# K0, K1 and Q0 on two DMA queues, weights' high words scaled in place, emission by data labels, first layer's units set between the weights' conversions

## The chip, the cores and the metric

The kernel runs on one core of a Trainium2 chip. Its engines run side by side, each through its own list of instructions in order: PE (TensorE, matmuls), DVE (VectorE), ACT (ScalarE), POOL (GpSimd) and SP (SyncE, which here issues DMAs). The metric is the device time of one execution in microseconds (us), lower is better. Three runs of the kernel before took 696.23, 696.32 and 696.54 us; the median is 696.32.

## What is computed

A delta-rule recurrence over 768 tokens, for 32 independent heads of 48 columns, followed by a feed-forward layer with a gate.

```python
k_n = k / (np.linalg.norm(k, axis=-1, keepdims=True) + 1e-06)
for t in range(S):                                  # S = 768, 32 heads, D = 48
    y[:, :, t] = np.einsum('bhd,bhde->bhe', q[:, :, t], state)
    v_old = np.einsum('bhde,bhd->bhe', state, kt)
    state = state + bt[:, :, :, None] * np.einsum('bhd,bhe->bhde', kt, vt - v_old)
...
h = x @ w_in                                        # 3072 x 384 @ 384 x 2048
sp = np.where(h > 20.0, h, np.log1p(np.exp(np.minimum(h, 20.0))))
g = h * np.tanh(sp)
return (g @ w_out).astype(np.float32)               # @ 2048 x 384
```

The two weight matrices come as 64-bit floats. They are read as pairs of 32-bit words and are turned on the chip into two f32 parts each (a high part and a remainder).

## The kernel before

The 768 tokens are cut into 12 chunks (n = 0 to 11) of 64. For each chunk the heads' recurrence is solved in closed form by small matmuls, and the chunk's output, 256 rows of 384, then goes through the feed-forward layer. A chunk's layer is called unit n here; it has eight pieces (fp = 0 to 7) of 18 matmuls `h<-x,wi` (L575), eight steps of the gate that alternate between ACT and DVE (L588 to L595), and 12 matmuls `acc<-wo,g` (L610).

Work ahead of a unit:

- `early(g)` for two chunks 2g and 2g+1: K is loaded (`ksrc`), transposed on DVE into `kt` (L264), multiplied with itself on PE (`pg`, L283), masked into `d` (L286), transposed into `gt` (L294); norms and the factor nb follow (L302 to L328), and then a triangular inverse is built row by row on DVE, for the groups g = 0 and 1 in 14 pairs of multiply (`pr`, L336) and add (`gt`, L338). It ends in three rows, `gt` times `bp` (L340) and the transposes `tt` (L345) and `tu` (L349).
- `merge(n)` for n up to 3: it joins two 16-row halves of the inverse, with PE matmuls `ma` (L375) and `mb` (L386), ACT copies `ym`, a DVE add (L389) and a transpose `tn` (L391).
- the stages of chunk n (all matmuls at L433): `gq`, `ta`, `tb`, `pz`, `py`/`ps`, each of them evacuated by ACT or DVE before the next. `turn_q` (L421) brings Q in transposed. The state of a chunk goes from `ps` into the next one.
- `turn(n)` transposes the chunk's output (`xt`, L548) into the layer's input x, of a high part (ACT, L550) and a remainder (DVE, L552). The first `h` of unit n waits for x.

The weights are 28 parts (12 `ri` of 128x1024 words, 16 `ro` of 128x768). `convert` takes for each: an ACT row that reads the high words (L219), four DVE rows (L221 to L227), the ACT rounding (L230), two PE matmuls for the remainder (`loi` or `loo`, L238 and L241) and the ACT copy of it (L243).

The order of emission is a plan: each generator is put into a heap with times from the table TN, and the piece with the least time is emitted next. Up to time 90 of the plan the framework's own scheduler sets the order in which each engine's instructions stand; from then on PE's order is that of the plan. All loads are issued by SP, in one order. K0 is loaded before K1, and Q0 goes into the buffer of K1 after it is transposed. In the trace the first `h` of units 0, 1, 2 and 3 start at 98.5, 170.2, 237.2 and 284.6 us; the stretches between these times are called stages below.

Of the kernel before, what the change touches and what calls it, by code (L numbers as in the profile page):

```python
# [10 lines left out]
F32 = mybir.dt.float32  # L11
# [9 lines left out]
F64_LEAST = 2.0 ** -15  # L21
F64_MOST = 122879.9921875
# [7 lines left out]
def bcast_in(ap, n):  # L30

    return ap.unsqueeze(2).broadcast_to([ap.shape[0], ap.shape[1], n])


@with_exitstack
def kernel(
# [40 lines left out]
    P = 128  # L77
# [28 lines left out]
    def put(gen, *times):
        for t in times:
            heappush(plan, (t, next(count), gen))

    def one(f, *a):  # L110
        f(*a)
        yield
# [8 lines left out]
    def defer(wait, f, *a):  # L121
        put(one(f, *a), now[0] + wait)
# [44 lines left out]
    loaded = []  # L167

    def load(dst, src):

        m = nc.sync.dma_start(out=dst, in_=src)  # L171
# [12 lines left out]

# [17 lines left out]
    identr = mp.tile([P, NCH, UT], F32R, tag="x0", name="identr", bufs=2)[:, 0, 0:P]  # L202
    spare = mp.tile([P, NCH * UT], F32, tag="x1", name="spare", bufs=2)[:, :512]
    nc.vector.tensor_copy(identr, ident)

    def convert(kind, i):
# [4 lines left out]
        if k % 3 < 2 or k >= 21:  # L211
# [7 lines left out]
        nc.scalar.activation(a, high.bitcast(F32), AF.Abs, scale=2.0 ** -80)  # L219
        yield  # L220
        nc.vector.tensor_scalar(a, a, F64_LEAST * 2.0 ** -80, F64_MOST * 2.0 ** -80, op0=ALU.max, op1=ALU.min)  # L221
# [599 lines left out]
```

## Time and profile before

| | |
|---|---|
| median of three runs | 696.32 us (696.23 to 696.54) |
| span of the profiled execution | 694.4 us, so about 1.9 us of the time lies around it |
| PE, DVE, ACT, POOL busy | 92%, 69%, 63%, 7% of the span |
| HBM moved | 31.56 MB read, 4.72 MB written |

The profile lists, for one execution, when each instruction started and how long it took, and the idle time before it with what ended it. "issue" is idle time for which the profile shows no other instruction to wait for. PEclk is the granted share of the PE clock. In a row "x60" counts records, and a matmul on 32-bit floats leaves two records each.

### The profile page before, as it was taken

To read this page: it belongs to the slowest core of one execution; us is meant where nothing else is said; L and a number is where in the kernel's file an instruction comes from. 1 tells how busy PE (TensorE), PEld (TensorE's weight loads), DVE (VectorE), ACT (ScalarE), POOL (GpSimd) and SP (SyncE) were. 2 spreads that over 40 slices of the span, in tenths; PEclk is the share of its full clock that TensorE was granted. 3 is DMA by queue.
4 is the path that set the end of the run, shared out by engine and by line. 5 is a ranking of instruction groups with operands and counts; after the bars stand their busy time and mean duration, and the time that the engine had idled before them with its cause. 6 is when DMAs were issued, how large, how long until landed. Compare 5 with 4: busy or idle time off the path is not lost.

```text
span 694.4 us, 23260 instructions
## 1 busy us (share of the span) xinstructions
PE 636.3 (92%) x10163; PEld 584.6 (84%) x10163; DVE 478.3 (69%) x1048; ACT 440.0 (63%) x821; POOL 48.8 (7%) x84
## 2 busy tenths in 40 slices
PE   6543899889979899999999999999999999999997
PEld 3313776779879899999899999999999999999997
DVE  4795278995449986579984699965899745453442
ACT  1350368775635766866758857568667587777674
POOL 5000000100101001000010010010000100000000
PEclk9565589999899999999999999999999999999999
DMA  5999230113041341231322403312222121000000
GB/s 82 227 247 348 39 59 14 21 17 59 18 62 25 45 70 32 33 66 26 48 47 36 70 15 48 59 33 33 44 35 43 19 37 35 13 19 8 1 24 24
DMA packets 160934, 37.79 MB, mean 54 GB/s; under 512 B 154176, under 2 KB 157248, under 8 KB 160832
## 3 DMA queue, kind: packets, MB, share of 16 engines
q1 hardware_dynamic: 160832, 36.30, 26.6%
q8 instruction: 80, 1.31, 0.8%
q14 instruction: 22, 0.18, 0.1%
HBM read 31.56 MB, written 4.72 MB: 52 GB/s over the span
## 4 chain that ended last, share of the span: by engine, by line
PE 45%; DVE 25%; ACT 13%; issue 6%; SPq 6%; DMA 3%; POOL 0%; DVEq 0%; ACTq 0%; POOLq 0%
PE h L575 16%; PE acc L610 15%; SPq L171 6%; DVE e L593 4%; PE gq L433 3%; ACT e L591 3%; DVE g L595 3%; DVE pr L336 3%; DVE gt L338 2%; ACT e L590 2%; ACT e L592 2%; PE py L433 2%; DVE e L589 2%; DVE xx L421 2%; DVE xx L480 2%
## 5 line engine op out<-in xcount | busy, mean ns | idle before, releaser
L575 PE MATMUL h<-x,wi 128*128 128x256 f32 x1728 | 228.6, 286 | 4.3 <-DVE e L593 3.5
L575 PEld LDWEIGHTS h<-x,wi 128*128 128x128 f32 x1728 | 215.9, 190 | 10.5 <-DVE e L593 2.8
L610 PE MATMUL acc<-wo,g 128*128 128x384 f32 x1152 | 222.1, 342 | 0.3 <-issue 0.3
L610 PEld LDWEIGHTS acc<-wo,g 128*128 128x128 f32 x1152 | 199.2, 189 | 3.8 <-issue 0.7
L593 DVE SCALAR_TENSOR_TENSOR e<-e,h 128x512 f32<-128x512 f32 x96 | 65.8, 686 | 97.0 <-ACT e L592 93.7
L590 ACT ACTIVATE e<-e 128x512 f32<-128x512 f32 x96 | 60.6, 631 | 73.2 <-DVE e L589 72.8
L594 ACT CAST g<-e 128x512 fp32r<-128x512 f32 x96 | 59.5, 620 | 41.2 <-DVE e L593 40.6
L595 DVE TENSOR_TENSOR g<-e,g 128x512 fp32r<-128x512 f32 x96 | 65.2, 679 | 20.6 <-ACT g L594 19.4
L588 ACT ACTIVATE e<-h 128x512 f32<-128x512 f32 x96 | 57.1, 595 | 30.8 <-PE h L575 30.0
L591 ACT ACTIVATE e<-e 128x512 f32<-128x512 f32 x96 | 60.5, 631 | 2.6
L592 ACT ACTIVATE e<-e 128x512 f32<-128x512 f32 x96 | 60.6, 632 | 2.4
L589 DVE TENSOR_SCALAR e<-e 128x512 f32<-128x512 f32 x96 | 40.8, 425 | 26.5 <-ACT e L588 26.2
L338 DVE TENSOR_TENSOR gt<-gt,pr 128x84 f32<-128x84 f32 (+14 forms) x148 | 46.1, 311 | 3.2
L336 DVE TENSOR_TENSOR pr<-gt 128x84 f32<-128x84 f32 (+14 forms) x148 | 46.0, 311 | 2.5
L433 PE MATMUL gq<-xx,kt 64*64 64x112 f32 (+1 forms) x768 | 45.2, 266 | 0.9 <-ACT wo L243 0.9
L433 PEld LDWEIGHTS py<-xx 128*64 128x64 f32 x768 | 39.1, 143 | 6.5 <-issue 2.8
L480 DVE TENSOR_TENSOR xx<-gq,amask 64x256 f32<-64x256 f32 x96 | 40.1, 418 | 4.6 <-PE gq L433 3.9
L433 PE MATMUL py<-xx 128*64 128x48 f32 x768 | 43.2, 230 | 0.0
L433 PEld LDWEIGHTS gq<-xx,kt 64*64 64x64 f32 x768 | 38.6, 141 | 2.6 <-issue 1.2
L414 POOL TENSOR_TENSOR vt<-vt,ne 128x384 f32<-128x384 f32 x24 | 21.0, 880 | 278.1 <-DVE ne L328 123.3
L433 PE MATMUL pz<-vt,tt 64*64 64x48 f32 x768 | 38.3, 236 | 2.4 <-ACT tt L462 1.3
L433 PEld LDWEIGHTS pz<-vt,tt 64*64 64x64 f32 x768 | 34.7, 140 | 6.4 <-ACT tt L462 2.8
(112 smaller groups left out, 717.9 us busy)
## 6 DMA issues: line engine op xcount, KB each, us to landing
ri<-in_moe_w_in_dram SPq DMA_DIRECT2D x12, 512.0 KB, 5.5
ro<-in_moe_w_out_dram SPq DMA_DIRECT2D x16, 384.0 KB, 6.0
vt<-in_v_dram SPq DMA_DIRECT2D x48, 96.0 KB, 2.8
xx<-in_k_dram SPq DMA_DIRECT2D x48, 96.0 KB, 2.8
out_dram<-o SPq DMA_DIRECT2D x48, 96.0 KB, 2.9
qsrc<-in_q_dram SPq DMA_DIRECT2D x48, 64.0 KB, 2.5
ksrc<-in_k_dram SPq DMA_DIRECT2D x44, 64.0 KB, 2.8
qsrc<-in_q_dram SPq DMA_DIRECT2D x48, 32.0 KB, 2.4
```

Of the source, the lines that this page charges most:

```text
L336: nc.vector.tensor_tensor(out=pv, in0=nj, in1=xj, op=ALU.mult)
L338: nc.vector.tensor_tensor(out=below, in0=below, in1=pv, op=ALU.add)
L433: last[:] = [nc.tensor.matmul(*a, start=True, stop=True)]
L575: nc.tensor.matmul(h[:, f2, :], wt["i", f * P // WI * NCH + c][:, i2, f0:f0 + P], x[:, c, :], start=(i == 0), stop=(i == 3 * NCH - 1))
L588: for d, f in ((0.7, lambda: nc.scalar.activation(e, h, AF.Exp, scale=-1.0)), (0.55, lambda: nc.vector.tensor_scalar(e, e, EXP20, 1.0, op0 ...
L590: (0.65, lambda: nc.scalar.activation(e, e, AF.Square)),
L591: (0.65, lambda: nc.scalar.activation(e, e, AF.Ln, bias=0.5, scale=0.5)),
L592: (0.7, lambda: nc.scalar.activation(e, e, AF.Exp, scale=-1.0)),
L593: (0.8, lambda: nc.vector.scalar_tensor_tensor(e, e, -1.0, h, op0=ALU.add, op1=ALU.mult)),
L594: (0.7, lambda: nc.scalar.copy(out=gg[:, 0], in_=e)),
L595: (0.8, lambda: eng.tensor_tensor(out=gg[:, 1], in0=e, in1=gg[:, 0], op=ALU.subtract))):
L610: nc.tensor.matmul(acc[t], gg[:, a, f2, ts_], wt["o", f][:, i2, :], start=(f == 0 and i == 0), stop=(f == NF - 1 and i == 2))
```

## The change

- **Two queues.** `load_src` puts half of the DMAs of K0, K1 and Q0 on ACT's queue, half stay on SP's. Q0 has a buffer of its own, `q0`, and is loaded straight after K1, before beta. The load of ACT's function table comes after these 12 DMA issues on ACT. The first weights are loaded behind beta and no longer between K0 and K1.
- **High words scaled in place.** `convert`'s first ACT row multiplies the high words by 2^-112 where they lie; the clamp on DVE then reads them there, every second word, from both sides (-F64_MOST to F64_MOST); the sign is merged by other bit operations. There are still an ACT row and four DVE rows for each part.
- **Emission by labels.** A piece of the plan can name data that it needs (`need`) and gives a label when its data is made (`give`); a piece whose needs aren't there is held until the label comes. TT holds new times of single pieces. Up to time 122 of the plan all five engines now stand in the plan's order.
- **Units between conversions.** Unit 0's pieces are put at `u0(fp)`, times that follow the conversions of the parts they read. `merge(1)` comes after unit 0 has begun. K2's and K3's `kt` come later, among the conversions. `early(0)`'s steps have no conversion between them.
- **Small ones.** 107 `warm` matmuls on zeros (before 23) keep PE at work; the identity is made first on POOL; all memsets of `ksrc` and `qsrc` are on DVE; `ym0` lies in the place of the last weight part; `tu` is transposed ahead of `tt` in groups 0 and 1; in chunk 0 `gq` takes the `acc` banks of PSUM; chunk 1's second `pz` and chunk 2's first `gq` are separate stages.

The core of the diff:

```diff
+    'early2': [118.5, 147.9, 150.3, 155.1, 164.7, 165.034, ...
+    'cv0': [None, 37.464, 38.114, 38.764, 39.414, 40.164, 40.964, 41.564],
...
-              d0=["k0",1,"k1","b",3,"q",3,"v","x",4,"k2",4,"k3",13],
-              us=[76., 140., 192., 242.],
-              warm=[(0.5,14),(16.5,3),(18.,6)],
+              fixed=((122.,('PE','DVE','Activation','Pool','SP')),(1e9,('PE',))),
+              d0=["k0","k1","q","a","b",3,"v","x",4,"k2","k3",7,"p",14],
+              us=[49., 136., 184., 232.],
+              warm=[(0.5,13),(8.0,2),(11.5,66),(27.9,2),(29.5,4),(30.6,4),(32.2,2),(36.4,4),(40.2,3),(42.1,2),(43.6,2),(46.6,3)],
...
-        m = nc.sync.dma_start(out=dst, in_=src)
-        if loaded and len(loaded) < TN.get('lo', 150):
-            order(m, loaded[-1])
-        loaded.append(m)
+        m = (nc.scalar if turns[0] else nc.sync).dma_start(out=dst, in_=src)
...
-    def load_src(dst, src, n):
+    def load_src(dst, src, n, both=False):
         for hh in range(2):
+            turns[0] = both and hh == 1
...
-        nc.scalar.activation(a, high.bitcast(F32), AF.Abs, scale=2.0 ** -80)
-        yield
-        nc.vector.tensor_scalar(a, a, F64_LEAST * 2.0 ** -80, F64_MOST * 2.0 ** -80, op0=ALU.max, op1=ALU.min)
+        nc.scalar.mul(out=high.bitcast(F32), in_=high.bitcast(F32), mul=2.0 ** -112)
+        yield
...
+        nc.vector.tensor_scalar(a, high.bitcast(F32), -F64_MOST, F64_MOST, op0=ALU.max, op1=ALU.min)
         yield
         nc.vector.tensor_scalar(ai, ai, 3, None, op0=ALU.logical_shift_left)
         yield
-        nc.vector.scalar_tensor_tensor(ai, high, 0x7FFFFFFF, ai, op0=ALU.bitwise_or, op1=ALU.bitwise_and)
+        nc.vector.scalar_tensor_tensor(ai, high, -0x80000000, ai, op0=ALU.bitwise_and, op1=ALU.bitwise_or)
...
+    def u0(fp):
+        return when(7 * (fp // 2) + 2.9 + 2.8 * (fp % 2)) + TN['ul']
...
-        put(one(units[n][0], fp), us(n + (fp + 0.25) / NFP))
+        put(f"g1.{n}.{fp}", one(units[n][0], fp), us(n + (fp + 0.25) / NFP) if n else u0(fp),
+            need=[f"X{n}.{t}" for t in range(2)] + [f"Wi{fp * 2 * P // WI * NCH + c}" for c in range(NCH)])
...
     def run(until):
         while plan and plan[0][0] < until:
-            now[0], _, gen = heappop(plan)
-            next(gen, None)
+            piece = heappop(plan)
+            now[0], _, gen, *at_piece[:2] = piece
+            lacks = [x for x in needs[gen] if x not in given]
+            if lacks:
+                waiting.setdefault(lacks[0], []).append(piece)
+                continue
+            at_piece[2] = 0
+            needs[gen] = next(gen, None) or ()
```

What stands where, at three places. DVE in the middle of `early(0)`'s steps (`pr` and `gt`); `mi` and `spare` are conversions of weights. Before:

```order
L221 TENSOR_SCALAR mi_808<-mi_808 128x512
L227 SCALAR_TENSOR_TENSOR mo_739<-ro_261,mo_739 128x384
L338 TENSOR_TENSOR gt_414<-gt_414,pr_3_458 128x2x12x3
L223 TENSOR_SCALAR mi_808<-mi_808 128x512
L336 TENSOR_TENSOR pr_4_461<-gt_414 128x88
L221 TENSOR_SCALAR spare<-spare 128x512
L225 SCALAR_TENSOR_TENSOR mi_808<-ri_273,mi_808 128x512
L338 TENSOR_TENSOR gt_414<-gt_414,pr_4_461 128x2x11x4
```

The same steps of the change on DVE, from the first one on:

```order
L410 TENSOR_TENSOR pr_1_506<-gt_482 128x28
L412 TENSOR_TENSOR gt_482<-gt_482,pr_1_506 128x2x14
L410 TENSOR_TENSOR pr_2_509<-gt_482 128x52
L412 TENSOR_TENSOR gt_482<-gt_482,pr_2_509 128x2x13x2
L410 TENSOR_TENSOR pr_3_512<-gt_482 128x72
L412 TENSOR_TENSOR gt_482<-gt_482,pr_3_512 128x2x12x3
```

The conversions have left this place; the first of them now stands behind the evacuation of chunk 0's first `gq`.

PE at chunk 0's stages before: `merge(1)` (its `ma` and `mb`) and a conversion's remainder (`loi`) stand between `pz` and the first `py`.

```order
L433 MATMUL pz_1_862<-vt_1_266,tt_106 64x48 x15
L375 MATMUL ma_0_884<-tu_501,d_165 32x16 x18
L375 MATMUL ma_1_920<-tu_501,d_165 32x16 x32
L238 MATMUL loi_955<-spare,ident 128x512
L241 MATMUL loi_955<-wi_953,identr 128x512
L386 MATMUL mb_0_961<-tt_106,ym_503 32x16 x32
L386 MATMUL mb_1_996<-tt_106,ym_503 32x16 x32
L433 MATMUL py_0_1036<-xx_98 64x48 x2
```

PE of the change behind unit 0's first piece `h_0`, where `merge(1)` now stands:

```order
L665 MATMUL h_0_1028<-x_0_1005,wi_986 128x256
L301 MATMUL loo_1056<-mo_1015,identr 128x384
L304 MATMUL loo_1056<-wo_1054,identr 128x384
L454 MATMUL ma_0_1062<-tu_556,d_177 32x16 x32
L454 MATMUL ma_1_1097<-tu_556,d_177 32x16 x32
L465 MATMUL mb_0_1135<-tt_111,ym_115 32x16 x32
L301 MATMUL loo_1173<-spare,identr 128x384
L304 MATMUL loo_1173<-wo_1171,identr 128x384
L465 MATMUL mb_1_1181<-tt_111,ym_115 32x16 x32
L665 MATMUL h_1_1225<-x_0_1005,wi_836 128x256
```

So `merge(1)` went from ahead of chunk 0's `py` to between the first two pieces of unit 0, and the remainders of weight parts stand around it.

DVE right behind the remainder of x for unit 0, in the change (`x_0` is the layer's input, `e_0` the gate's first piece):

```order
L641 TENSOR_TENSOR x_0_1006<-xt_1_1011,x_0_1005 128x3x128
L288 SCALAR_TENSOR_TENSOR mo_1015<-ro_265,mo_1015 128x384
L290 SCALAR_TENSOR_TENSOR mo_1015<-ro_265,mo_1015 128x384
L284 TENSOR_SCALAR spare<-ro_267 128x384
L286 TENSOR_SCALAR spare<-spare 128x384
L288 SCALAR_TENSOR_TENSOR spare<-ro_267,spare 128x384
L680 TENSOR_SCALAR e_0_1047<-e_0_1047 128x512
```

At this place before, fourteen conversions had been begun; now five have, so more of the conversions stand behind unit 0's start. From x of unit 0 to x of unit 1 DVE's list had 57 conversion rows, 30 rows of `early(1)`'s steps and 4 transposes of Q; it now has 94 conversion rows, 10 of those steps, 8 transposes of Q and two transposes `kt`.

More of the change, by code (lines that the diff above doesn't have):

```diff
@@ L97, with put, give, do @@
     po = ctx.enter_context(tc.tile_pool(name="po", bufs=1, space=PSUM))
-    nc.scalar.preload_act_table_set("natural_log_exp_and_others")
-    plan, now = [], [0.0]
+    lead = tc.manual_schedule(engines={getattr(mybir.EngineType, e) for e in TN['fixed'][0][1]})
+    lead.__enter__()
+    plan, now, at_piece = [], [0.0], [None, 0, 0]
     count = iter(range(10 ** 9))
[L106 to L110, printed above, removed]
+    needs, given, waiting = {}, set(), {}
+    def put(key, gen, *times, need=()):
+        own = TT.get(key, ())
+        needs[gen] = need
+        for j, t in enumerate(times):
+            heappush(plan, (own[j] if j < len(own) and own[j] is not None else t, next(count), gen, key, j))
+    def give(*labels):
+        for x in labels:
+            given.add(x)
+            for t, c, *rest in waiting.pop(x, ()):
+                heappush(plan, (max(t, now[0]), c, *rest))
+    def do(t, f, *a, need=()):
+        put(f"{f.__name__}{a}".replace(" ", ""), one(f, *a), t, need=need)
+    def one(f, *a, label=None):
         f(*a)
+        if label:
+            give(label)
         yield
@@ L119, in tensor, with defer @@
         tensor_free[0] = now[0] + dur
-    def defer(wait, f, *a):
-        put(one(f, *a), now[0] + wait)
+    def defer(wait, f, *a, need=(), label=None):
+        at_piece[2] += 1
+        put("{}.{}>{}".format(*at_piece), one(f, *a, label=label), now[0] + wait, need=need)
     def spread(t0, t1, n):
         return [t0 + (t1 - t0) * (i + 0.5) / n for i in range(n)]
+    eye = mp.tile([P, 512], F32, tag="e", name="eye")[:, :P]
+    make_identity(nc, eye)
+    identr = cp.tile([P, P], F32R, name="identr")
+    nc.vector.tensor_copy(identr, eye)
+    ident = identr.bitcast(F32)
     ksrc = cp.tile([P, NP, 2, 32], F32, name="ksrc")
@@ L461, in out @@
                 r = slice(64 * hh, 64 * hh + 32)
-                nc.scalar.copy(out=tt[r, :, 32:], in_=ps[r])
+                (nc.vector.tensor_copy if hh and n < TN['ev'] else nc.scalar.copy)(out=tt[r, :, 32:], in_=ps[r])
         for p in range(NP):
@@ L534, in s_y @@
                 yield mm(py[64 * hh:64 * hh + 64, p, :], x[:, p, hh, D:D + C], x[:, p, hh, 0:D],
-                         then=(lambda: defer(2.1, out)) if end and hh and n == NS - 1 else None)
+                         then=(lambda: defer(2.1, out, label=f"Y{n}{h}")) if end and hh and n == NS - 1 else None)
             for hh in (1, 0) if n < NS - 1 else ():
@@ L538, in s_y @@
                 yield mm(ps[r0:r0 + D, p, :], x[:, p, hh, D + C:], x[:, p, hh, 0:D],
-                         then=(lambda: defer(2.1, out)) if end and hh == 0 else None)
+                         then=(lambda: defer(2.1, out, label=f"Y{n}{h}")) if end and hh == 0 else None)
     def transposed(n, y):
@@ L677, in loads @@
             elif x == "q":
-                load_src(qsrc, qq, 0)
+                load_src(q0, qq, 0, both=True)
             elif x == "v":
@@ L789 @@
             run(until)
+    assert not plan and not waiting, waiting
 _INS = ['q', 'k', 'v', 'beta', 'moe_w_in', 'moe_w_out']
```

261 lines of the change are left out of this document (180 added, 81 removed).

## The prediction

> **What bounds the kernel now.** I read first the table of engines and the clock, then each stage apart, then the chain of waits. The share of PE over the span (92%) hides that two thirds of the kernel are full and the first third is not, so the stages come first. Columns are stretch, its length, busy time of PE, PEld, DVE, ACT, POOL with records, granted clock, DMA share, GB/s.
>
> ```profile
> core 0: us, PE busy (x) PEld busy (x) DVE busy (x) ACT busy (x) POOL busy (x), PEclk, DMA share, GB/s
> 0.00:98.50 98.50, 60.88 (x1221) 41.39 (x1222) 59.00 (x136) 32.18 (x66) 16.71 (x36) 0.65 0.67 171
> 98.50:170.20 71.70, 65.04 (x1132) 54.80 (x1130) 63.37 (x152) 53.96 (x109) 3.97 (x6) 1.00 0.21 30
> 170.20:237.20 67.00, 60.38 (x1348) 56.59 (x1336) 44.33 (x104) 34.56 (x67) 5.86 (x9) 0.92 0.26 42
> 237.20:284.60 47.40, 47.37 (x823) 45.47 (x824) 33.95 (x69) 33.33 (x61) 4.17 (x6) 1.00 0.27 44
> 284.60:694.40 409.80, 402.58 (x5657) 386.33 (x5655) 277.67 (x589) 285.96 (x521) 18.08 (x27) 1.00 0.19 34
> ```
>
> From unit 3 on PE is busy 402.58 of 409.80 us and the change leaves the times of those units' pieces alone: **that part stays**. The gain has to come out of the first 284.6 us. To unit 1's start DVE works 59.0 + 63.4 = 122.4 of 170.2 us, mostly on conversions, and all 28 parts are converted by then both before and after the change. So unit 1 can't start long before 122 us whatever is done, and the question is how much of DVE's 48 us of idle time goes.
>
> **Stage 1, to the first `h` of unit 0 (98.5 us).** The start, in order of time (start, duration, engine, instruction, idle before and its releaser):
>
> ```profile
> 0.81 4.10 SPq L171 DMA_DIRECT2D ksrc<-in_k_dram  x8
> 2.15 0.48 DVE L628 MEMSET zero<- 128x512 f32 x1 [0.15 <-issue]
> 2.69 7.43 PE L635 MATMUL warm<-zero 128*128 128x512 bf16 x23 [2.69 <-DVE zero L628]
> 6.92 1.25 DVE L264 STREAM_TRANSPOSE kt<-ksrc 128x1024 f32<-128x1024 f32 x1 [4.29 <-DMA ksrc<-in_k_dram]
> 8.20 1.46 DVE L156 COPY xx<-ident 64x384 f32<-64x384 f32 x4
> 10.05 1.99 PE L283 MATMUL pg<-kt 64*32 64x64 f32 x128
> 21.81 0.42 DVE L286 TENSOR_TENSOR d<-pg,lmask 128x256 f32<-128x256 f32 x1
> 22.48 1.91 DVE L294 STREAM_TRANSPOSE gt<-d 128x1024 f32<-128x1024 f32 x1
> 36.90 0.19 DVE L336 TENSOR_TENSOR pr<-gt 128x28 f32<-128x28 f32 x1
> 51.53 0.27 DVE L336 TENSOR_TENSOR pr<-gt 128x112 f32<-128x112 f32 x1
> 55.47 0.69 DVE L340 TENSOR_TENSOR gt<-gt,bp 128x512 f32<-128x512 f32 x1
> 56.20 1.90 DVE L345 STREAM_TRANSPOSE tt<-gt 128x1024 f32<-128x1024 f32 x1
> 57.96 0.99 DVE L349 STREAM_TRANSPOSE tu<-gt 128x512 f32<-128x512 f32 x1
> ```
>
> K0 costs 4.10 us of issue on one queue; on two, half, so it lands some 2 us sooner. DVE then has five memsets (0.48 each) and the four copies (1.46) ahead of `kt`; these end near 5.9, so `kt` moves from 6.92 to 5.9 only. K1 behind K0, no longer behind a weight, lets the second `kt` follow at once. Two `pg` (1.99 each, the first half on the first K), two masks (0.4) and `kt` (1.25) then put `gt` at 5.9 + 1.25 + 1.0 + 0.4 + 1.25 + 2.0 + 0.4 = 12.2, and with some 2 for the waits between them 14.4 (was 22.48).
>
> From `gt` to the first step the same path is seen undisturbed later, in the chain that ended last:
>
> ```profile
> 303.18 1.98 DVE gt L294
> 308.95 1.22 DVE gt L321
> ```
>
> That is 5.8 us to L321; with its tail I take 6.6, so steps from 21.0 (was 36.90, with conversions between). From 51.53 to 55.47 seven pairs ran alone in 3.94 us, 0.56 each: 14 pairs are 7.9, so 28.9. Then `bp` 0.7, `tu` 1.0, `tt` 2.0: **32.6, where `tt` and `tu` ended at about 58.9 before (`tt` at 58.1)**. That is 25.5 us of the forecast, and it comes from taking the conversions out of the steps.
>
> What follows, to 98.5, took 40.4 us:
>
> ```profile
> 65.56 1.36 PE L386 MATMUL mb<-tt,ym 32*32 32x16 f32 x83 [3.93 <-issue]
> 81.70 1.57 PE L375 MATMUL ma<-tu,d 16*32 16x16 f32 x100
> 83.19 2.08 PE L238 MATMUL loi<-spare,ident 128*128 128x512 f32 x2
> 85.63 1.91 PE L386 MATMUL mb<-tt,ym 32*32 32x16 f32 x128
> 92.91 0.72 PEld L433 LDWEIGHTS py<-xx 128*64 128x64 f32 x21 [0.94 <-DVE xx L421]
> ```
>
> And three stretches of that stage, with the columns of the first table:
>
> ```profile
> 0.00:10.00 10.00, 7.31 (x23) 2.73 (x23) 4.30 (x9) 1.55 (x2) 8.93 (x24) 1.00 0.68 113
> 10.00:50.00 40.00, 20.58 (x281) 10.98 (x280) 31.44 (x75) 16.44 (x34) 3.19 (x7) 0.68 0.82 209
> 80.00:90.00 10.00, 10.00 (x315) 8.24 (x315) 3.03 (x7) 4.00 (x9) 1.21 (x2) 0.50 0.01 3
> ```
>
> Off this path go `merge(1)`'s `ma` and `mb` (3.9 with its wait), `loi` ahead of `mb` (2.4), the remainder and the Q transposes ahead of the second `py` (2.4), and half clock on `pz` and `py` (2.5, if the `warm` rows hold the clock): 11.2, so 29.2 left. The wait of 3.93 for "issue" is kept, as nothing names its cause: if it is tied to the loads of that time it goes (-5.5 with a second one behind it), if chunk 0's stages are as slow as before it is +11. The 84 more `warm` lie where PE waits for DVE's steps: at the 0.32 of the row above (7.43 / 23) the 66 that follow the second `pg` take 21 us and end by 32, when `tu` and `tt` are made, and I take them as hidden. A third slower, at a low clock, they end near 40 and hold `ma` up by 7. Twelve DMA issues go to ACT ahead of its table, 0.51 each by the row above, 6.2 in all; ACT had 1.55 us of work in the first 10, and the norms come near 15, so they cost nothing. **First `h`: 32.6 + 29.2 = 62** (bounds 56, without the two waits, and 73, with chunk 0's stages as before).
>
> The row of 80 to 90 us has PE busy 10.00 of 10 at a granted clock of 0.50. The Trainium skill, "TensorE: Matmul & The Clock Gate", section "What's actually happening", says that the clock is halved by default and is released after one busy window of some 3.4 us. The trace disagrees for small matmuls: 10 busy us of tiles of 16 to 64 rows didn't release it. By the page's rule chunk 0's stages would run at full clock with or without the new `warm`; by the row they do so only if groups of 2 to 4 `warm` (128 rows, 512 columns) count, and where they don't, stage 1 is 2.5 us longer.
>
> **Stage 2, to the first `h` of unit 1 (71.7 us).** DVE is the fullest engine beside PE there, and gets more. Rows of the groups by form (busy, mean ns of one, idle before):
>
> ```profile
> L225 DVE SCALAR_TENSOR_TENSOR mo<-ro,mo 128x384 int32<-128x384 int32 x12 | 6.6, 554 | 0.1
> L227 DVE SCALAR_TENSOR_TENSOR mo<-ro,mo 128x384 int32<-128x384 int32 x12 | 6.6, 549 | 0.0
> L221 DVE TENSOR_SCALAR mo<-mo 128x384 f32<-128x384 f32 x12 | 4.2, 354 | 1.8 <-ACT mo L219 1.7
> L223 DVE TENSOR_SCALAR mo<-mo 128x384 int32<-128x384 int32 x12 | 4.3, 355 | 0.1
> L225 DVE SCALAR_TENSOR_TENSOR mi<-ri,mi 128x512 int32<-128x512 int32 x9 | 6.1, 679 | 0.1
> L227 DVE SCALAR_TENSOR_TENSOR mi<-ri,mi 128x512 int32<-128x512 int32 x9 | 6.1, 678 | 0.1
> L221 DVE TENSOR_SCALAR mi<-mi 128x512 f32<-128x512 f32 x9 | 3.8, 423 | 2.0 <-ACT mi L219 2.0
> L223 DVE TENSOR_SCALAR mi<-mi 128x512 int32<-128x512 int32 x9 | 3.8, 418 | 0.1
> L219 ACT ACTIVATE mi<-ri 128x512 f32<-128x512 f32 x9 | 6.0, 669 | 8.9 <-DMA ri<-in_moe_w_in_dram 7.6 <-PE loo L238 1.2
> L421 DVE STREAM_TRANSPOSE xx<-qsrc 64x512 f32<-64x512 f32 x48 | 33.8, 705 | 2.9 <-PE py L433 1.5
> ```
>
> A part of `ro` costs DVE 1.81 us, one of `ri` 2.20, a row 0.49 on average. Between x of unit 0 and x of unit 1 there are 37 conversion rows more (57 to 94): +18.1. Four more transposes of Q (0.705): +2.8. Two `kt`: +2.5. Twenty fewer step rows (0.27): -5.4. `tt` and `tu` gone: -3.0. The other rows nearly cancel: +0.5. Together +15.5; by the share that sums of rows had in this stage (63.4 busy against 68.2 summed, since neighbours overlap) +14.6, so DVE 78 us. Its idle 8.3 us shrink a little where conversions fill them: **85 us** (was 71.7). ACT has by the same count some 70, PE 77 (nine more remainders, `merge(1)`), so DVE ends it.
>
> The clamp keeps its 0.42 in this sum. It reads every second word now; the nearest rows of another price are those of the same 512 columns at 0.68 (L225), which would be 0.26 x 23 parts, +5 in the stage, and below nothing I see no reason. Since both are one instruction over the same columns I stay with 0.42. "VectorE: DVE Perf Modes" of the Trainium skill, section "What auto-detection actually checks", gives an operation of one source with both ends in SBUF two 32-bit elements a cycle, with no condition on the stride; by it the +5 doesn't come. No run here shows that yet.
>
> The scaling in place is one ACT row like L219 (0.67) in its place: no cost. It must wait for its own load, as L219 did (7.6 us of its idle was for the load); with parts converted later the loads are long there, and that wait goes.
>
> **Stages 3 and 4 (67.0 and 47.4 us).** Steps that left stage 2 go here, DVE 44 to 54 of 64, so PE ends them. PE's rows for stage 3 come to 59.7 at full clock; before it had 0.92 and 6.6 us idle, and I take 4 of idle: **64**. Stage 4 gets 10 us of DVE's steps beside 34 busy in 47: **48.5**.
>
> **Sum.** 62 + 85 + 64 + 48.5 = 259.5 where 284.6 stood; 409.8 is added: span 669. The execution had 1.9 us around its span (694.4 against 696.32, the median): **671**.
>
> **Rivals.**
>
> - *Conversions paced by three in-order engines.* A part goes ACT, DVE, ACT, PE, ACT, and all five engines now stand in the plan's order up to 122. If DVE is as idle in stage 2 as it was between 10 and 50 us (31.44 of 40), 78 us of work take 99: 14 more, **685**. For it: every first DVE row of a part waits for ACT (L221, releaser L219). Against: only 3.8 us in all.
> - *A late start.* `warm` at half clock or chunk 0's stages as slow as before: first `h` at 73 to 75, **684**.
> - *PE's floor.* PE has 77 + 59.7 + 47.4 + 402.6 us of work behind the first `h`; with that at 56 and stages 2 and 3 nearly full: 56 + 79 + 60 + 48 + 409.8 + 1.9, **655**.
> - *Slower than before.* The remainder of a part (PE, 1.04 at full clock from L238's 2.08) and its ACT copy (0.67, as L219) aren't covered, because ACT's next scaling stands in order behind the copy and DVE's next clamp behind the scaling. 23 parts stand behind unit 0's start; 1.7 each is 39 us, **710**. It decides from 25 / 23 = 1.1 us a part. Against it: before, with parts in flight side by side, DVE lost 3.8 us at L221.
> - *It doesn't do what it says.* Unit 0 starts early but its pieces wait for their parts, so only the end of the conversions counts; this is in the sum, as unit 1 starts at 147 for 170. If that end doesn't move at all, the time is **696**.
>
> **How the numbers follow.** Forecast (664 to 678) 0.60; paced conversions 0.15; late start 0.11; PE's floor 0.05; no change 0.03; slower 0.06. The two middle rivals are both near 685, so the range goes from 656 to 690 and leaves about 0.13 out. About 1.4 us (0.2%) is what a measurement of this kernel tells from no change. Faster 0.91, same 0.03, slower 0.06.
>
> **What would show it.** Right: `kt` near 6 us, steps of `early(0)` from 21 to 29 without a gap, first `h` of units 0 to 3 near 62, 147, 211 and 260, DVE over nine tenths busy between the first two, PEclk 1.00 in stage 1's second half, no load among the releasers of ACT's scaling. Wrong: DVE under 80% busy in stage 2 with ACT as its releaser (paced conversions), `ma` waiting behind `warm` or PEclk 0.50 at `pz` (late start), the clamp at 0.6 or more, or units behind the fourth longer than 47.4.

## The result, and the profile after

The changed kernel takes 689.92 us (four runs, 688.32 to 690.37) where the kernel before takes 696.43 beside it: a ratio of 0.990, with a 95% interval of 0.987 to 0.992. It is faster, by 6.5 us, where 25 were forecast. The profiled execution has a span of 688.0 us. Its first `h` rows of units 0, 1, 2 and 3 start at 61.7, 162.1, 227.1 and 278.1 us (before 98.5, 170.2, 237.2, 284.6).

The stages of the changed kernel, with the columns of the prediction's first table:

```profile
core 0: us, PE busy (x) PEld busy (x) DVE busy (x) ACT busy (x) POOL busy (x), PEclk, DMA share, GB/s
0.00:61.70 61.70, 49.53 (x1009) 29.91 (x1021) 42.52 (x91) 23.10 (x46) 14.22 (x33) 0.94 0.77 174
61.70:162.10 100.40, 84.03 (x1191) 65.94 (x1192) 81.08 (x174) 63.28 (x127) 5.56 (x8) 0.90 0.29 78
162.10:227.10 65.00, 61.42 (x1559) 57.80 (x1558) 44.53 (x103) 34.68 (x68) 5.17 (x8) 0.95 0.26 41
227.10:278.10 51.00, 48.98 (x825) 46.93 (x824) 42.90 (x96) 33.23 (x62) 5.14 (x7) 0.97 0.34 55
278.10:688.00 409.90, 402.43 (x5657) 386.35 (x5655) 277.69 (x589) 285.13 (x520) 19.08 (x28) 1.00 0.19 34
```

| stretch | before | forecast | after |
|---|---|---|---|
| to the first `h` of unit 0 | 98.5 | 62 | 61.7 |
| to that of unit 1 | 71.7 | 85 | 100.4 |
| to that of unit 2 | 67.0 | 64 | 65.0 |
| to that of unit 3 | 47.4 | 48.5 | 51.0 |
| to the end | 409.8 | 409.8 | 409.9 |

So unit 0 starts 36.8 us sooner, and unit 1 only 8.1 us sooner. Unit 0 runs stretched over the conversions, a piece every 11 to 18 us, and the conversions end nearly where they did: the copy of the last part's remainder (ACT L243 before, L306 now) is over at 157.9 us before and 153.9 after.

In the second stretch DVE is busy 81.08 of 100.4 us, PE 84.03, ACT 63.28. **No engine is full.** The longest waits of DVE in that stretch, without the one for x of unit 0 at its edge (engine and line, for whom, us in total, how often, the longest), are these:

```profile
DVE e L684 <- ACT e L683: 4.6, 5, 1.4
DVE e L680 <- ACT e L679: 3.4, 3, 1.9
DVE d L359 <- PE pg L356: 3.4, 3, 1.6
DVE tt L468 <- PE mb L465: 2.0, 1, 2.0
DVE g L686 <- ACT g L685: 1.5, 2, 1.2
DVE vt L562 <- issue: 1.0, 1, 1.0
```

The first, second and fifth are steps of unit 0's gate, 9.5 us together: DVE stands in the plan's order, a gate step is next, and ACT hasn't made its input; where conversion rows stand behind the step, they wait with it. The timeline of DVE around unit 0's start shows the same with numbers (start, duration, row, idle before and its releaser):

```profile
54.70 0.36 DVE L284 TENSOR_SCALAR mo<-ro 128x384 f32<-128x384 f32 x1 [0.68 <-PE loi L301]
61.31 0.56 DVE L641 TENSOR_TENSOR x<-xt,x 128x384 fp32r<-128x384 f32 x1 [6.25 <-ACT x L639]
61.78 0.35 DVE L286 TENSOR_SCALAR mo<-mo 128x384 int32<-128x384 int32 x1
...
69.92 0.53 DVE L288 SCALAR_TENSOR_TENSOR mo<-ro,mo 128x384 int32<-128x384 int32 x1
70.38 1.23 DVE L327 STREAM_TRANSPOSE kt<-ksrc 128x1024 f32<-128x1024 f32 x1
73.60 0.29 DVE L468 TENSOR_TENSOR tt<-tt,mb 128x128 f32<-128x128 f32 x1 [2.00 <-PE mb L465]
73.92 0.71 DVE L470 STREAM_TRANSPOSE tn<-tt 128x512 f32<-128x512 f32 x1
74.56 0.52 DVE L290 SCALAR_TENSOR_TENSOR mo<-ro,mo 128x384 int32<-128x384 int32 x1
```

The conversion of `mo` that began at 54.70 waits 6.25 us behind x of unit 0, and the one of 69.92 gets its last row 4.6 us later, behind a `kt`, an add of merge(1) that waits for PE, and `tn`.

PE shows what that does. The chain of work that ended last, followed back from unit 1's first `h`, has in this stretch 53.3 us of PE, 26.3 of DVE, 15.8 of ACT and 4.7 of "issue" (its 195 longest pieces, added up by engine). In the same stretch of the kernel before it had 51.5 of PE, 11.2 of DVE and 5.2 of ACT. **PE's part is the same; 26 us of DVE and ACT have come to stand in series with it.** A piece of that chain, in order of time (start, duration, engine and line):

```profile
111.33 0.64 ACT e L683
111.99 0.69 DVE e L684
112.68 0.61 DVE mi L288
113.29 0.02 issue
113.32 0.70 DVE mi L290
114.02 0.14 issue
114.15 1.10 PE loi L301 x2
115.25 0.28 PE loi L304
115.53 2.16 PE h L665 x18
```

A gate step on ACT lets DVE's gate step go, behind which a part's last two rows stand; those let PE make the remainder, and only then can unit 0's next `h` run.

The fourth stretch is 2.5 us over the forecast, in one place. DVE and PE at 260 us:

```profile
259.80 2.03 DVE L419 STREAM_TRANSPOSE tt<-gt 128x1024 f32<-128x1024 f32 x1
...
261.67 2.02 DVE L432 STREAM_TRANSPOSE tn<-gt 128x1024 f32<-128x1024 f32 x1
...
263.72 0.69 DVE L684 SCALAR_TENSOR_TENSOR e<-e,h 128x512 f32<-128x512 f32 x1
...
264.47 1.90 PE L665 MATMUL h<-x,wi 128*128 128x256 f32 x8 [2.02 <-DVE e L684]
```

The gate's step L684 stands behind the two transposes that end `early(2)`; `h` waits 2.02 us for it, and the granted clock goes to 0.5 for 3.4 us from 265 us on.

### The profile page after: what moved, and what is told of

Its sections match the earlier page's. It is cut to its first block, busy times and chain, and to the rows that moved or that the text cites. A ratio compares the mean times of both kernels' runs of the same rounds, so it can differ in the third digit from the quotient of the medians.

```text
span 688.0 us, 23366 instructions
## 1 busy us (share of the span) xinstructions
PE 646.4 (94%) x10235; PEld 586.9 (85%) x10247; DVE 488.7 (71%) x1050; ACT 439.4 (64%) x821; POOL 49.2 (7%) x84
## 4 chain that ended last, share of the span: by engine, by line
PE 43%; DVE 25%; ACT 15%; SPq 6%; issue 5%; DMA 5%; ACTq 0%; DVEq 0%
PE h L665 16%; PE acc L702 15%; SPq L233 6%; DVE e L684 4%; DVE g L686 3%; ACT e L682 3%; ACT e L681 3%; ACT e L683 2%; DVE xx L565 2%; DVE pr L410 2%; DVE gt L412 2%; PE gq L515 2%; DVE e L680 2%; DMA ksrc<-in_k_dram 2%; DVE xx L502 1%
## 5 line engine op out<-in xcount | busy, mean ns | idle before, releaser
L665 PE MATMUL h<-x,wi 128*128 128x256 f32 x1728 | 233.1, 290 | 4.9 <-DVE e L684 4.0
L665 PEld LDWEIGHTS h<-x,wi 128*128 128x128 f32 x1728 | 221.2, 194 | 10.6 <-DVE e L684 3.9
L684 DVE SCALAR_TENSOR_TENSOR e<-e,h 128x512 f32<-128x512 f32 x96 | 65.8, 686 | 86.0 <-ACT e L683 80.1
L686 DVE TENSOR_TENSOR g<-e,g 128x512 fp32r<-128x512 f32 x96 | 65.5, 683 | 21.5 <-ACT g L685 20.5
L412 DVE TENSOR_TENSOR gt<-gt,pr 128x84 f32<-128x84 f32 (+14 forms) x148 | 47.8, 323 | 3.8
L410 DVE TENSOR_TENSOR pr<-gt 128x84 f32<-128x84 f32 (+14 forms) x148 | 47.2, 319 | 2.9
L515 PEld LDWEIGHTS py<-xx 128*64 128x64 f32 x768 | 37.6, 138 | 6.1 <-issue 4.0
L515 PE MATMUL gq<-xx,kt 64*64 64x112 f32 (+1 forms) x768 | 42.2, 256 | 0.0
L515 PE MATMUL py<-xx 128*64 128x48 f32 x768 | 41.2, 224 | 0.0
L515 PEld LDWEIGHTS pz<-vt,tt 64*64 64x64 f32 x768 | 32.1, 133 | 6.4 <-issue 3.5
L515 PE MATMUL ps<-xx 128*48 128x48 f32 x704 | 37.5, 208 | 0.0
L515 PEld LDWEIGHTS gq<-xx,kt 64*64 64x64 f32 x768 | 36.5, 133 | 0.5 <-issue 0.4
L515 PE MATMUL pz<-vt,tt 64*64 64x48 f32 x768 | 35.5, 228 | 0.8 <-ACT tt L547 0.6
```

Of the source, the lines that this page charges most:

```text
L410: nc.vector.tensor_tensor(out=pv, in0=nj, in1=xj, op=ALU.mult)
L412: nc.vector.tensor_tensor(out=below, in0=below, in1=pv, op=ALU.add)
L515: last[:] = [nc.tensor.matmul(*a, start=True, stop=True)]
L665: nc.tensor.matmul(h[:, f2, :], wt["i", f * P // WI * NCH + c][:, i2, f0:f0 + P], x[:, c, :], start=(i == 0), stop=(i == 3 * NCH - 1))
L684: (0.8, lambda: nc.vector.scalar_tensor_tensor(e, e, -1.0, h, op0=ALU.add, op1=ALU.mult)),
L686: (0.8, lambda: eng.tensor_tensor(out=gg[:, 1], in0=e, in1=gg[:, 0], op=ALU.subtract))):
```

## The experiments

Three theories stood at first for the second stretch. *DVE paces*: the stretch is DVE's 81 us of work and what can't be filled. *Clock*: the half-clock windows (PEclk 0.90) stretch PE's part of the chain. *Order* or *handover*: the engines wait for each other in a fixed order, and none of them alone sets the length. A last one came with the runs: *a fixed block* (merge(1) among the conversions) holds the parts up.

One thing has to be known for reading them. Behind plan time 122 the order of DVE, ACT and POOL is made by the framework's scheduler, and it can come out otherwise when something ahead of it changes: with only fewer `warm` matmuls, DVE's list is the same row by row until ten rows ahead of x of unit 1 and differs behind it. The third and fourth stretches together took 115 to 123 us in most of these kernels (116.0 after the change, 127.8 and 125.3 in two). So the theories are judged by the second stretch and the start of unit 1, read in one profile of each kernel, and the times stand beside it. Two profiles of the changed kernel itself have unit 1 at 162.1 and 165.6 us, so a move of less than these 3.5 us shows nothing; the stretch is 100.4 and 100.3 us in them. The kernel before, run beside each group of kernels, took a median of 696.7 to 697.8 us.

First the changed kernel again, unchanged:

> The changed kernel as it is, beside the next three and on the chip of the runs so far, whose times lie above those of the first comparison: all theories, time 690 to 697, unit 0 at 62 to 66 us and unit 1 some 100 us later.

690.63 us, a ratio of 0.991 (0.988 to 0.994); first `h` of unit 0 at 65.3 and of unit 1 at 165.6 us. This is what the others are compared with, unless the first profile (61.7 and 162.1) is named.

| run | time, us | ratio to before (95%) | unit 0 | unit 1 | last copy |
|---|---|---|---|---|---|
| after_again | 690.63 | 0.991 (0.988 to 0.994) | 65.3 | 165.6 | 157.5 |
| hot | 698.7 | 1.003 (1.000 to 1.005) | 63.5 | 162.2 | 154.6 |
| less_dve | 698.36 | 1.002 (0.998 to 1.006) | 63.9 | 164.6 | 156.0 |
| less_pe | 695.18 | 0.999 (0.996 to 1.001) | 63.1 | 161.6 | 154.2 |
| pool_scale | 693.44 | 0.996 (0.994 to 0.998) | 67.4 | 166.8 | 157.5 |
| slow22 | 695.84 | 0.999 (0.996 to 1.002) | 64.2 | 161.7 | 152.2 |
| ab_late | 704.1 | 1.012 (1.009 to 1.015) | 64.3 | 166.9 | 162.6 |
| sched_pe | 705.04 | 1.015 (1.011 to 1.019) | 86.4 | 172.0 | 162.0 |
| u0_late | 716.63 | 1.030 (1.028 to 1.033) | 112.0 | 186.1 | 166.7 |
| fix50 | 706.73 | 1.014 (1.010 to 1.019) | 79.3 | 172.3 | 161.2 |
| fix62 | 691.6 | 0.992 (0.989 to 0.995) | 62.5 | 165.2 | 153.6 |
| fix90 | 691.21 | 0.992 (0.990 to 0.994) | 68.3 | 162.8 | 151.0 |
| lead15 | 690.84 | 0.991 (0.988 to 0.994) | 67.8 | 161.1 | 154.2 |
| lead30 | 694.02 | 0.995 (0.993 to 0.998) | 67.7 | 163.7 | 155.8 |
| lead45 | 697.71 | 1.001 (1.000 to 1.003) | 62.7 | 169.4 | 160.7 |
| warm_few | 699.23 | 1.003 (1.000 to 1.006) | 61.0 | 164.7 | 155.4 |
| less_all | 692.69 | 0.993 (0.990 to 0.996) | 62.1 | 156.7 | 152.4 |
| m1_early | 701.31 | 1.003 (0.999 to 1.006) | 78.1 | 171.7 | 165.5 |

### The clock

```diff
+            hot(ps[:, :256], {8: 16, 9: 16, 14: 24}.get(k, 0))
             nc.tensor.matmul(ps, ident, a, start=True, stop=False)
...
+            hot(h[:, 0, :], 24 if (n, fp) == (0, 0) else 0)
```

> The changed kernel with 96 more small matmuls on the identity's bits (256 columns, results overwritten) put where PE waits in stage 2: ahead of unit 0's first h, of the remainders of parts 8, 9 and 14, and of chunk 1's transposition. Theory 'clock': the five windows at a granted clock of 0.5 between 62 and 162 us (20 us in all) lengthen the PE rows of the chain; with the clock held, stage 2 goes from 100 to about 92 and the time from 690 to 682. Theory 'order' (each engine stands in one fixed order and waits for a row that isn't ready while ready rows stand behind it): PE has slack, the clock matters little, stage 2 stays within 2 us of 100.

Stage rows of the changed kernel run again and of this one:

```profile
65.30:165.60 100.30, 84.36 (x1190) 65.80 (x1191) 81.39 (x173) 63.10 (x127) 5.32 (x8) 0.90 0.29 78
```

```profile
63.50:162.20 98.70, 85.70 (x1266) 67.85 (x1264) 78.38 (x167) 62.50 (x127) 5.55 (x8) 0.95 0.28 76
```

The clock went from 0.90 to 0.95 and the stretch from 100.3 to 98.7. Half of the lost clock came back and brought 1.6 us, where 8 were forecast for all of it: the clock alone is worth little here, though it wasn't held at 1.00.

### Less work for one engine

```diff
-        nc.vector.tensor_scalar(ai, ai, 3, None, op0=ALU.logical_shift_left)
+        if k < 5:
+            nc.vector.tensor_scalar(ai, ai, 3, None, op0=ALU.logical_shift_left)
```

> The changed kernel without the shift on DVE (L286) for the 23 parts behind the fifth, so their weights are wrong: 23 rows of 0.39, 9.0 us less work for DVE and nothing else changed. Theory 'DVE paces stage 2' (its 81 us of work with idle time that can't be filled): unit 1 starts 8 to 10 us sooner, near 153, time 681. Theory 'a part's round trip DVE-PE-ACT paces': each part is 0.39 shorter only where DVE ends the wait, 3 to 5 us in all, time 686.

```diff
+            both = k < 5 or k % 2 == 0
+            if both:
-            nc.tensor.matmul(ps, ident, a, start=True, stop=False)
+                nc.tensor.matmul(ps, ident, a, start=True, stop=False)
```

> The changed kernel without the first remainder matmul (L301, on 32-bit floats) for every second part behind the fifth (11 parts), so their remainders are wrong: some 11 us less work for PE at the rows' 0.65 to 2.04. Theory 'DVE paces': unit 1 starts within 2 us of 162. Theory 'round trip': 1.0 less for each of these parts, and unit 1 starts 8 to 11 us sooner.

```diff
+        if k < 13:
             nc.scalar.mul(out=high.bitcast(F32), in_=high.bitcast(F32), mul=2.0 ** -112)
+        else:
+            nc.gpsimd.tensor_scalar(high.bitcast(F32), high.bitcast(F32), 2.0 ** -112, None, op0=ALU.mult)
```

> The changed kernel with the in-place scaling of the 15 parts behind the thirteenth on POOL, which is 7% busy, in place of ACT: 15 rows of 0.55, 8 us less work for ACT and none of its rows ahead of the gate. Theory 'order' (PE and DVE wait for ACT rows that stand behind these scalings): unit 1 starts 4 to 8 us sooner, 682 to 686. Theory 'DVE paces': within 2 us of 690. If POOL's rows slow DVE's beside them, later than before.

The second stretch in the three, in this order:

```profile
63.90:164.60 100.70, 82.61 (x1190) 64.28 (x1191) 72.83 (x153) 62.10 (x127) 5.32 (x8) 0.91 0.29 74
```

```profile
63.10:161.60 98.50, 75.31 (x1167) 61.88 (x1168) 79.86 (x171) 62.16 (x126) 5.85 (x8) 0.86 0.30 78
```

```profile
67.40:166.80 99.40, 80.63 (x1190) 63.20 (x1191) 84.56 (x177) 56.53 (x112) 26.68 (x23) 0.93 0.30 77
```

DVE lost 8.6 us of busy time, PE 9.1, ACT 6.6, and the stretch stays at 98.5 to 100.7. "DVE paces" is out, and so is any other single engine. What one engine no longer does becomes its idle time. In the second of them the granted clock is also lower, 0.86 for 0.90.

### The order

```diff
-    ab0=(39.5, 1.45)
+    ab0=(1000., 0.)
```

> The changed kernel with one number changed: ACT's in-place scaling of each part is set just ahead of the part's clamp, and no longer up to 40 us ahead of it. Theory 'order': between 80 and 91 us ACT was busy without a gap while PE waited, and six scalings of later parts stood there; without them unit 0's pieces come earlier, the conversions' end moves from 152 to about 146, time 684. Theory 'DVE paces' or 'clock': the same work in another place, within 2 us of 690, or later since a clamp now waits for its scaling (up to +8).

```diff
-    slow=1.4
+    slow=2.2
```

> The changed kernel with the steps of unit 0's gate set 2.2 apart for 1.4 in the plan, so on DVE and ACT more conversion rows stand between two of them. In stage 2 DVE waited 9.5 us for ACT's gate rows (L684, L680, L686). Theory 'order': most of that is filled, unit 1 starts 4 to 8 us sooner, 682 to 686. Theory 'DVE's waits only move to other rows': within 2 us of 690.

ab_late puts ACT's scaling right ahead of the clamp: DVE now waits 11.0 us for it (L284 behind L277: 4.4, 2.7, 2.6 and 1.3) and the parts end 5 us later. So the early scaling is right, against what I expected. Its waits for the gate fall at the same time, from 9.6 us (after_again) to 3.6, and the stretch is 102.6 us all the same. In slow22 the three waits for the gate fall to 5.8 us; unit 1 comes 3.9 us sooner than in after_again, but only 0.4 sooner than in the first profile, so a gain isn't shown, and the time is 5 us longer (stage 4 of 54.4). So shorter waits at the gate go with a longer stretch in the one and with one 2.8 us shorter (97.5) in the other.

```diff
-    fixed=((122.,('PE','DVE','Activation','Pool','SP')),(1e9,('PE',))),
+    fixed=((122.,('PE',)),(1e9,('PE',))),
```

> The changed kernel with only PE in the plan's order up to time 122; DVE, ACT, POOL and the load queue are ordered by the framework's scheduler. Theory 'order': ACT and DVE no longer stand behind rows that wait, stage 2 is 5 to 10 us shorter (680 to 685), provided stage 1 keeps its 62. Rival: the fixed order is what gives stage 1 its 62 us (conversions come back between the steps of early(0)); first h at 75 or later and the time 695 to 705.

The same line with 50.2, 62 and 90 in place of 122, and all five engines as they were:

> The changed kernel with all five engines in the plan's order only up to plan time 50.2, where unit 0's first piece is emitted, and PE alone from there on. Taking rows away from DVE, PE or ACT left stage 2 at 98 to 101 us, while with DVE, ACT and POOL ordered by the scheduler 22 parts took 66.8 us (3.04 each) for 82.8. Theory 'order' (the fixed order makes each engine wait for the others in turn): first h stays near 63, the parts come every 3.0 to 3.2 us, stage 2 is 80 to 90 and the time 672 to 682. Rival 'the start is to blame' (parts come at 3.0 only after a late first h, since more rows of them are done by then): stage 2 stays near 100, time within 3 us of the changed kernel.

> As the run before it with the fixed order up to plan time 62, which takes in merge(1) and unit 0's first two pieces. Theory 'order': between the two, stage 2 of 85 to 95, time 675 to 686. Rival: within 3 us of the changed kernel.

> The same up to plan time 90: most of the conversions (20 of 28) stand in the fixed order. Theory 'order': a third of the gain at most, stage 2 of 93 to 98. Rival: within 3 us of the changed kernel.

Without the fixed order the parts do come faster once they run: from the seventh part's copy to the last one, 2.7 us a part in sched_pe (105 to 162 us) and 2.8 in fix50, against 3.5 in the changed kernel (83 to 157.5). But the seventh comes 19 to 21 us later, the first `h` 14 to 21, and unit 1 at 172. In fix62 the first `h` is at 62.5 and the parts come at 2.9, yet the seventh only at 92 and unit 1 at 165.2. The work is the same; the scheduler only puts other rows first. In fix90 the stretch is 94.5 us, within the range of 'order', but it begins at 68.3 and unit 1 starts at 162.8, so nothing is gained. A simple loss by the plan's order is out too.

### Unit 0 out of the way, merge(1) out of the way

```diff
-        return when(7 * (fp // 2) + 2.9 + 2.8 * (fp % 2)) + TN['ul']
+        return 104.0 + 3.0 * fp
```

> The changed kernel with unit 0's eight pieces behind the conversions (plan times 104 to 125 for 49 to 100). Theory 'unit 0 and the conversions share DVE, ACT and PE, and only their sum counts': the conversions end earlier, near 130 for 152, unit 0 ends later, and unit 1 starts within 6 us of 162. Theory 'a part's round trip DVE-PE-ACT paces them': the conversions keep 3.8 us a part and end near 150, unit 0 follows them, unit 1 starts near 180, time 705.

Neither. The seventeenth part is copied at 113 us for 120 (116 in the first profile), so that unit 0's absence brings the conversions some 3 to 7 us by then; but the rest of them stand among unit 0's pieces, the last is copied at 166.7, and unit 1 starts 20.5 us later. Unit 0 set between the conversions is worth that: most of it runs beside them.

```diff
-    m1=(53,53.5,54.5,55.5)
+    m1=(38.6,39.4,40.4,41.4)
```

> The changed kernel with merge(1) ahead of chunk 0's stages, as in the kernel before (plan times 38.6 to 41.4 for 53 to 55.5). In all runs so far the sixth to seventh part took 7 to 12 us, where merge(1) stands with a wait of PE of 2.5 us and one of DVE of 2.0. Theory 'fixed block': the parts behind it come 4 to 6 us sooner and unit 1 near 157 to 160, while the first h comes 3 to 4 us later as the forecast took it (3.9 for merge(1)). Theory 'handover': what moves out of stage 2 comes into stage 1, unit 1 stays within 2 us of 163 and the time within 3 us of 690.6.

The seventh part follows the sixth by 4.5 us for 8.4 (copies at 86.4 and 90.9 us, and at 74.3 and 82.7): the block is real. But the first `h` comes at 78.1, 13 us later and not 4. The profile's chain of waits of that run, from 33 to 78 us, lies on SP's queue (45.6%) and on loads of `ri` (41.0%). It doesn't show that the loads set the start: SP issues the same three loads of `ri` from 57.54 us on in the changed kernel and from 57.69 on here. From 44 to 78 us ACT's list shows no wait for a load, only these for PE:

```profile
ACT at L531 <- PE ta L515: 10.2, 1, 10.2
ACT wi L306 <- PE loi L304: 7.1, 2, 3.7
ACT ym L456 <- PE ma L454: 5.6, 2, 3.0
ACT xx L587 <- PE pz L515: 3.7, 2, 3.2
```

In the changed kernel, from 42 us to its first `h`, the first, second and fourth are 7.7, 1.8 and 0.5 us, and the third isn't there. So `merge(1)`, set ahead of chunk 0's stages, makes ACT wait for PE at other rows too, and the granted clock is 0.72 from 35 to 78 us (0.92 from 35 to 61.7 in the changed kernel). How the 13 us divide between the two isn't shown.

### More lead for DVE's conversion rows

```diff
+        if i >= 4:
+            ts = [t - 1.5 for t in ts]
```

> The changed kernel with DVE's four conversion rows of the parts behind the fourth set 1.5 earlier in the plan (the rows of PE and ACT stay), about half a part of lead. Theory 'handover' (stage 2 is a chain that goes from DVE to PE to ACT and back because each part is made just before it is used; no engine alone paces it): PE and ACT find their words ready more often, and the 6.3 us for which DVE stood before x of unit 0 (L641) with conversions behind it are partly filled; unit 1 starts 3 to 5 us sooner, 686 to 688. Rival (DVE's lead doesn't matter, a fixed block such as merge(1) or the loads holds up the parts): within 3 us of 690.6.

> The same with 3.0, about one part of lead, in which parts 4 and 5 stand ahead of x of unit 0. Theory 'handover': 5 to 9 us sooner, 681 to 686, with less DVE on the chain of stage 2 than its 27 us and DVE's idle time there under 15 us. Rival: within 3 us of 690.6.

> The same with 4.5. There are three buffers for the words in conversion, so DVE can't be more than three parts ahead of PE. Theory 'handover': as with 3.0 or slightly less, since DVE then waits for a buffer and unit 0's gate rows come later. Rival: within 3 us of 690.6.

```profile
67.80:161.10 93.30, 77.45 (x1190) 59.82 (x1190) 78.85 (x168) 61.17 (x126) 5.90 (x8) 0.98 0.27 67
```

That is lead15: the stretch is 93.3 us, the shortest with a first `h` ahead of 70, unit 1 at 161.1, and DVE's wait at x of unit 0 goes from 6.3 to 3.5 us. The time is that of the changed kernel (690.84). More lead is worse: at 3.0 unit 1 comes at 163.7 and the time is 694.02; at 4.5 DVE waits for buffers and loads (L284 waits 7.4 us for PE's remainders, 5.9 for ACT's rounding, 3.0 for a load of `ro`), and unit 1 comes at 169.4. The first `h` of lead15 is 2.5 to 6.1 us later than in the two profiles of the changed kernel, and its unit 1 is 4.5 us sooner than in one of them and 1.0 sooner than in the other, so a gain isn't shown.

### Fewer `warm`

```diff
-              warm=[(0.5,13),(8.0,2),(11.5,66),(27.9,2),(29.5,4),...
+              warm=[(0.5,13)],
```

> The changed kernel with 13 matmuls on zeros in place of 107. By the forecast's terms chunk 0's stages run at half clock then, which cost 2.5 us: first h near 65 to 66 for 62 to 65, time 693. If the clock of chunk 0's stages is worth what it was in the kernel before (40.4 us from tt to the first h, of which 11.2 were taken off): up to 75 and 700. If unit 1's start hangs on the conversions' end and not on unit 0's start, the time is within 3 us of 690.6 whatever the first h does.

```profile
0.00:61.00 61.00, 34.27 (x928) 25.15 (x928) 42.34 (x91) 22.99 (x46) 14.28 (x33) 0.78 0.76 171
```

In it the clock is at 0.50 for 27 us:

```profile
21.00:48.00 27.00, 13.05 (x451) 11.81 (x451) 22.03 (x55) 7.85 (x15) 3.06 (x5) 0.50 0.80 195
```

The first `h` comes at 61.0 all the same, as early as with them. The 94 matmuls do nothing for the start: the half clock lies beside DVE's steps and chunk 0's first stages, and from 48 us on, where `pz` and `py` stand, the clock is 1.00 without them. Unit 1 stays too (164.7). The median is 8.6 us longer; in the profiles 5.5 to 6 us of that lie in the third and fourth stretches (68.3 and 53.7, for 65.5 and 51.0 in after_again), where DVE's order is another one.

### Less work for three engines at once

The edits of less_dve and pool_scale, and that of less_pe for every part behind the fifth.

> The changed kernel with three removals together for the parts behind the fifth: no shift on DVE (L286), no first remainder matmul on PE (L301), and from the fourteenth part the scaling on POOL for ACT; so the weights are wrong. Singly they moved stage 2 by +0.5, -1.8 (for every second part) and -0.8 us. Theory 'handover': the chain holds some 14 us of L301, 1.2 of L286 and 1.8 of L277 rows, and with all three gone no other engine's row takes their place at once: stage 2 is 8 to 14 us shorter, 86 to 92. Rival 'a fixed block holds the parts up': within 3 us of 100.

```profile
62.10:156.70 94.60, 71.27 (x1144) 63.04 (x1145) 70.92 (x137) 55.16 (x111) 27.67 (x23) 0.80 0.32 85
```

PE has 13.1 us less to do, DVE 10.5, ACT 7.9 (POOL 22 more), and the stretch is 5.7 us shorter: between the two forecasts. The part of the whole run's chain that lies in this stretch says what took the place: PE's share falls to 24.4 us, and beside it stand 30.1 of DVE, 15.7 of ACT, 11.2 of POOL (the moved scaling), 6.6 of "issue" and 6.3 of a load of `ro`. And the clock is granted at 0.80.

## Why the prediction was right and wrong

**The start was right in sum.** Steps from 21.0 to 28.9 and `tt` at 32.6 were forecast; the steps start at 21.3 and `tt` ends at 33.8, and the first `h` is at 61.7. Some terms were not, and that the sum fits to 0.3 us is luck, as their errors cancel:

```profile
4.87 3.52 DVE L217 COPY xx<-identr 64x384 f32<-64x384 f32 x4
8.31 1.22 DVE L327 STREAM_TRANSPOSE kt<-ksrc 128x1024 f32<-128x1024 f32 x1
...
21.29 0.16 DVE L410 TENSOR_TENSOR pr<-gt 128x28 f32<-128x28 f32 x1
...
31.95 1.89 DVE L419 STREAM_TRANSPOSE tt<-gt 128x1024 f32<-128x1024 f32 x1
```

The four copies took 3.52 us where 1.46 was taken from the kernel before, so `kt` is at 8.3 and not 5.9, later than before: K0 on two queues brought nothing to it, for DVE wasn't ready. The waits behind it were shorter than the 2 us put in. What stood behind `tt` took 27.9 us for 29.2. The 2.5 us for half clock were put down to the `warm` rows, and that isn't so: without them `pz` and `py` have the full clock as well, and the first `h` is as early. By the rule in "TensorE: Matmul & The Clock Gate" of the Trainium skill, section "What's actually happening", they would have been needless among chunk 0's stages; here they were. But the clock didn't follow the rule: in warm_few PE was busy, as the profile counts it, for 3.50 of 3.50 us from 37.7 to 41.2 at a clock of 0.50, and the full clock came only at 48. Nor can the prediction's row of 80 to 90 us be put down to small tiles: `loi` with its 128 rows (L238 and L241) takes 2.5 of the ten us, from 83.19 on, and `py` has 128 rows too. What frees the clock stays open. Nor is merge(1)'s term confirmed: back in its old place it costs 13 us and not 3.9, with more waits of ACT for PE.

**The second stretch is where the prediction failed, in one step**: "Its idle 8.3 us shrink a little where conversions fill them". DVE's work was sized well (78 forecast, 81.1 measured; the clamp kept its price, below). Its idle time was put at 7 us and is 19.3. The premise was that a list with more ready rows leaves fewer gaps; but an engine takes its list in order, and gate steps that wait for ACT (9.5 us) and rows that wait for PE (`d` 3.4, the add of merge(1) 2.0) stand in it. That these waits are there is shown. That they set the length is not: with the gate's waits down to 5.8 us (slow22) the stretch is 97.5, and with 3.6 (ab_late) it is 102.6. PE was put at 77 us and was busy 84.03, at a clock of 0.90; "so DVE ends it" doesn't hold either, as no engine is full and 8.6 us less work on DVE left the stretch where it was. The rival of three in-order engines named this, took DVE's share from the start of the kernel before (79%; it is 81%) and came to 99 us for a measured 100.4 and 685 for 689.92. It had 0.15. Its number may be luck, since the share came from a stretch without a unit in it. What it had wrong is the place: it looked at the clamp's wait for ACT's scaling, which doesn't show among the waits, and the longest of them are at the gate.

**What the prediction also took wrongly** is that the stretches add up. Unit 1's start was written as unit 0's start plus 85. In the runs unit 0's first `h` lies between 61 and 112 us, and unit 1's between 157 and 186: starts 13 to 21 us later (m1_early, fix50, sched_pe) moved unit 1 by 6 to 7. My sentence that unit 1 can't start long before DVE's 122 us was the better frame: DVE had worked 123.6 us by then, and its idle time went from 48 to 38.5, not to 25.

**The clamp** with a stride of two words:

```profile
L284 DVE TENSOR_SCALAR mo<-ro 128x384 f32<-128x384 f32 x12 | 4.2, 349 | 0.7 <-PE loi L301 0.7
L284 DVE TENSOR_SCALAR mi<-ri 128x512 f32<-128x512 f32 x9 | 4.2, 467 | 0.0
```

0.349 for 0.354 and 0.467 for 0.423 us: no price that matters, as the rule in "VectorE: DVE Perf Modes" of the Trainium skill, section "What auto-detection actually checks", would have it; the 0.044 more of the longer form is not explained by it.

**Stages 3 and 4**: 65.0 for 64, and 51.0 for 48.5. The ten more us of DVE's steps in stage 4 were counted and said to fit beside 34 in 47; DVE was full to 260 us, and the gate fell behind two transposes.

**What stays open.** That no single engine and not the plan's order as such sets the 100 us is shown, and that the clock is at most a small part of it. What does set it stays open. That several chains of nearly the same length run beside each other is what less_all suggests, and doesn't show: 31 us of work taken from PE, DVE and ACT (8 of them moved to POOL, which needs 22) for 5.7. Which of them would have to be cut together to get the forecast's 85 isn't settled; no version here was faster than the changed kernel.

## What to carry to other kernels

When work is moved into the gaps of another stage, don't cost the gaps as fillable: an engine takes its list in order, and a gap belongs to the row that waits in it. A first guess is to take the busy share that the engine reached in a stage where the same rows ran, and to divide by it; here that gave 99 us for 100.4, which is one case and may be luck. And ask for the end of the work that the next unit needs (here the conversions, 158 to 154 us) before counting an earlier start as gain.

## What the runs showed of the hardware that wasn't expected

- Work taken from PE went with a lower clock: with PE's busy time at 84, 75 and 71 us in the second stretch (after_again, less_pe, less_all), the granted clock was 0.90, 0.86 and 0.80. That the one makes the other isn't shown: in lead15, with the same work as in after_again in another order, it was 0.98.
- The same COPY of 64x384 f32 took 0.354 us on average in the kernel before and 0.869 in the changed one, where its four stand at 4.9 us beside POOL's memsets of the start (two took 1.05 and 1.10 us, two 0.66). In the kernel before they stood beside other rows of POOL (L143 and L145) and took 0.35, so POOL's being busy isn't enough. A step row at 23.93 us (L410, 128x108) took 0.87 for 0.27 beside POOL's multiply of `vt` (L494). Whether POOL is the cause wasn't tried.
- The scaling of 15 parts on POOL raised POOL's busy time in the second stretch from 5.3 to 26.7 us, about 1.4 us a row for ACT's 0.55 to 0.68.
